# Decode attention with a gated feed-forward: K turned by VectorE in 32-bit blocks instead of by TensorE, one V slot, one set a loop turn

## The chip, the core and the metric

The kernel runs on one core of a Trainium2 chip. Engines: PE is TensorE (PEld its weight loads), DVE VectorE, ACT ScalarE, POOL GpSimd, SP the engine that issues most transfers. The metric is the device time of one execution in microseconds (us), as the median over runs.

## The reference

One new token for each of four batch rows goes through attention over the last 4096 positions of a cache, and beside it through a ReLU-gated feed-forward; a sigmoid gate of the token mixes the two. All tensors are bfloat16.

```python
g = sigmoid((A_x * gate_w).sum(-1, keepdims=True))      # A_x: 4 x 1 x 512
q = (A_x @ A_wq) as 32 heads of 128                      # A_wq: 512 x 4096
k, v = last 4096 positions of A_k_cache, A_v_cache       # 4 x 8 heads x 16384 x 128
p = softmax(q . k * 128 ** -0.5)                         # 4 query heads share one k/v head
a = (p . v) @ A_wo                                       # A_wo: 4096 x 512
h = relu(A_x @ W_gate) * (A_x @ W_up)                    # 512 x 1792 each (the token is A_x)
b = h @ W_down                                           # 1792 x 512
out = g * a + (1 - g) * b
```

## The kernel before, in words

The attention is cut into eight sets: batch row b = s // 2 and four of the eight k/v heads. A set's K is 4 MB and lies in SBUF as 128 partitions of 32 KB; so does its V. Both have two slots (`Ksb[:, s % 2]`, `Vsb[:, s % 2]`), which the weights reuse: W_q in the second V slot at the start, W_gate and W_up in the first K slot and W_down in the first V slot at the end. W_o has a place of its own (`Wbig`).

SP issues all large transfers in one fixed order: W_q, K0, K1, V0, K2, V1, ..., K7, V6, W_gate, W_up, V7, W_down, W_o in five pieces. They are served first in, first out. A K load waits until the scores of the set two back have read its slot, a V load until the value products two back have.

For each set, the positions must come onto the partitions' other side, since scores contract over the 128 elements of a head. Two bf16 elements are taken as one 32-bit word, and PE turns the K of a set in 64 fp32 transposes of 128x128 words (L352), eight to a fill of a PSUM buffer; two buffers alternate, and ACT and DVE copy the fills back over K in SBUF (L357, L359). Then:

- scores (L373): 32 products of 512 columns in two halves, four abreast in 32-column groups of PE; DVE adds a mask and takes the row maximum (L383);
- maximum (L390, L395): one product brings the maxima of all partitions into one row, DVE reduces it;
- exponent (L403) on ACT over 128x2048, turn (L413): DVE transposes the weights in 32x32 blocks;
- values (L421): 64 products of 256 columns, four abreast; ACT copies the sums out (L430).

The softmax and the value products of set s-1 are interleaved by hand with the transposes and scores of set s. PE's program is a loop of four turns of two sets each (the first set of a turn carries the end of the set before), the other engines' programs are straight lists. After the loop come the last set's rest, `combine` (L440 to L448: sums over partitions, normalising), `gateup` and the feed-forward's elementwise steps (L457 to L470), and the products with W_down and W_o (L503), 256 columns each and two abreast, into one PSUM bank; DVE and ACT copy the result (L517, L518) and SP writes it.

Before the loop: the gate's sigmoid, the projection of the queries (L310: 32 products of 512 columns, four abreast), and the queries' layout (L320 to L340; L340 is POOL's copy of one set's queries).

Of the kernel before, what the change touches and what calls it, by code (L numbers as in the profile page):

```python
# [11 lines left out]
B = 4  # L12
D = 512
HQ = 32
HKV = 8
SK = 16384
DH = 128
# [5 lines left out]
SCALE = DH ** -0.5  # L23
NEG = -1.0e9
LOWEST = -3.0e38

NTR = 2
NPAIR = 2
NFILL = 8
WO_CUTS = (0, 16, 26, 30)  # L30
ACT_TAKES = (1, 3, 4, 6, 7)


class Program:

# [8 lines left out]
    def __init__(self):  # L44
        self.ops = {e: [] for e in self.ENGINES}
        self.events = {}
        self.counts = {}
        self.history = {}
        self.dmas = []
        self.turns = []  # L50
        self.shared = {}
# [37 lines left out]
    def per_turn(self):  # L89

        return self.lowered

    def emit_list(self, eng, sems, engine, ops, shift, seen):
        for fn, name, waits, is_dma in ops:
            for s, n in self.need(engine, waits).items():
# [10 lines left out]
    def signature(self, ops, shift):  # L106
        seen = {}
        out = []
        for fn, name, waits, is_dma in ops:
# [9 lines left out]
    def emit(self, engine, eng, sems):  # L119
        ops = self.ops[engine]  # L120
        if engine != "pe":
            self.emit_list(eng, sems, engine, ops, {}, {})
            return
        t = self.turns
        self.emit_list(eng, sems, engine, ops[:t[0]], {}, {})
        first = self.signature(ops[t[0]:t[1]], {})
        for k in range(1, len(t) - 1):
            shift = {s: k * n for s, n in self.lowered.items() if s not in self.shared}
            assert self.signature(ops[t[k]:t[k + 1]], shift) == first, k
# [5 lines left out]
        shift = {s: (len(t) - 1) * n for s, n in self.lowered.items() if s not in self.shared}  # L135
        self.emit_list(eng, sems, engine, ops[t[-1]:], shift, {})


def bass_gated_mix__sliding_block_cached__glu_gated_reglu__decode_kernel(
# [13 lines left out]
    with ExitStack() as ctx:  # L153
        def sb(name, shape, dt):
            return ctx.enter_context(nc.sbuf_tensor(name, shape, dt))

        Ksb = sb("Ksb", [128, 2, 16384], BF16)
        Vsb = sb("Vsb", [128, 2, 16384], BF16)
        Wbig = sb("Wbig", [128, 16384], BF16)
        sc = sb("sc", [128, 2, 2048], BF16)  # L160
        pT = sb("pT", [128, 2, 2048], BF16)
        qrow = sb("qrow", [128, 2, 1024], BF16)
        mask = sb("mask", [128, 1024], BF16)
        ident = sb("ident", [128, 128], BF16)
        identw = sb("identw", [128, 128], FP32)
        ones = sb("ones", [128, 128], BF16)
        onesf = sb("onesf", [128, 132], FP32)
        Wsel = sb("Wsel", [128, 132], FP32)
        Wsum = sb("Wsum", [128, 64], FP32)
        m4 = sb("m4", [128, 20], FP32)  # L170
        S32 = sb("S32", [128, 32], FP32)
        xsb = sb("xsb", [5, 512], BF16)
        xT = sb("xT", [128, 4, 32], BF16)
        xw = sb("xw", [5, 512], FP32)
        gwB = sb("gwB", [128, 512], BF16)
        gsb = sb("gsb", [128, 8], FP32)
        qW = sb("qW", [128, NSET, 2, 32], BF16)
        qS = sb("qS", [128, 2, 2, 32], BF16)
        mx = sb("mx", [128, 2, NPAIR], FP32)
        mrow = sb("mrow", [128, 128], FP32)  # L180
        qmask = sb("qmask", [128, 128], FP32)
        negmax = sb("negmax", [128, 2], FP32)
        rowsum = sb("rowsum", [128, NSET], FP32)
        osb = sb("osb", [128, NSET, 256], FP32)
        recip = sb("recip", [128, 4], FP32)
        rgate = sb("rgate", [128, 4], FP32)
        idle = sb("idle", [128, 2], FP32)
        oq = sb("oq", [128, 128], BF16)
# [396 lines left out]
```

## Time and profile before

| | |
|---|---|
| median of 3 runs | 196.26 us (196.18 to 196.35) |
| profiled execution, its own time | 196.16 us |
| its span | 194.9 us |
| PE busy | 129.2 us (66%), 1578 products |
| DVE busy | 73.8 us (38%) |
| ACT busy | 66.5 us (34%) |
| POOL busy | 11.7 us (6%) |
| read from HBM | 81.01 MB, 416 GB/s over the span |

The time of an execution is that of the runs; every row of the profile comes from the one profiled execution, and its span runs from the first to the last record. In a row of a group: line, engine, operation, what is written and read, shape, count, then busy time in us and mean ns of one, then the idle time of the engine just before them and what ended it. In a row of the timeline: start, length (both us), engine, line, operation. PEclk is the clock granted to PE, 1.00 being full.

### The profile page before, as it was taken

Reading aid. Unit: us, or ns where it says so; the run is one execution under the profiler, and the core shown is the slowest. Engines: PE = TensorE matmul, PEld = TensorE weight load, DVE = VectorE, ACT = ScalarE, POOL = GpSimd, SP = SyncE. Lnnn points to the kernel's source line nnn. Section 1 sums busy time; section 2 is a strip of 40 time slices with the busy share of each in tenths; the row PEclk is TensorE's granted clock in tenths of the full one; section 3 lists DMA queues with packets and bytes.
Section 4 is the critical chain, followed back from the end, with each engine's and each line's share of the span. In section 5 each row is a group of like instructions: output and inputs, shape, how many; then the busy total and the mean of one; then the engine's idle time right before and its main releaser. Section 6 shows DMA issues by size and latency. Waiting matters only on the chain.

```text
span 194.9 us, 3496 instructions
## 1 busy us (share of the span) xinstructions
PE 129.2 (66%) x1578; PEld 101.0 (52%) x1578; DVE 73.8 (38%) x95; ACT 66.5 (34%) x77; POOL 11.7 (6%) x43
## 2 busy tenths in 40 slices
PE   0137398788769649872887099649972987713964
PEld 0113396576556439651765097439651865503742
DVE  0200045259239323930682029324920492180000
ACT  2005025565255452435342424433435252510000
POOL 8820000000000000000000000000000000000000
PEclk9999999999999996999999859996999699995799
DMA  6999999999999999999999999999999999998992
GB/s 216 431 430 437 430 430 427 437 440 430 437 440 430 437 430 437 430 430 437 432 437 425 430 437 430 430 437 430 430 430 430 430 390 427 475 430 382 424 403 82
DMA packets 3881, 81.11 MB, mean 416 GB/s; under 512 B 409, under 2 KB 930, under 8 KB 1058
## 3 DMA queue, kind: packets, MB, share of 16 engines
q1 hardware_dynamic: 3864, 81.01, 97.3%
q8 instruction: 5, 0.08, 0.2%
q14 instruction: 2, 0.02, 0.0%
q10 hardware_dynamic: 10, 0.01, 0.0%
HBM read 81.01 MB, written 0.00 MB: 416 GB/s over the span
## 4 chain that ended last, share of the span: by engine, by line
DMA 59%; PE 21%; DVE 14%; ACT 3%; issue 1%; SPq 1%
DMA Ksb<-in_A_k_cache_dram 47%; PE TRT L352 15%; DMA Wbig<-in_A_wo_dram 12%; DVE Ksb L359 6%; DVE pT L413 5%; PE SCT L373 3%; DVE sc L383 3%; ACT Ksb L357 3%; PE OB L421 2%; PE SCT L503 1%; SPq L240 0%; PE FB L390 0%; SPq L533 0%; ACT outr L518 0%; SPq L235 0%
## 5 line engine op out<-in xcount | busy, mean ns | idle before, releaser
L352 PE MATMUL TRT<-identw,Ksb 128*128 128x128 f32 x512 | 75.1, 306 | 25.4 <-DMA Ksb<-in_A_k_cache_dram 17.5
L352 PEld LDWEIGHTS TRT<-identw,Ksb 128*128 128x128 f32 x512 | 65.9, 158 | 35.8 <-DMA Ksb<-in_A_k_cache_dram 18.8
L357 ACT COPY Ksb<-TRT 128x1024 f32<-128x1024 f32 x40 | 40.5, 1012 | 58.4 <-PE TRT L352 58.2
L359 DVE COPY Ksb<-TRT 128x1024 f32<-128x1024 f32 x24 | 29.4, 1223 | 40.1 <-PE TRT L352 40.1
L421 PE MATMUL OB<-Vsb,pT 128*32 128x256 bf16 x576 | 19.0, 288 | 7.5 <-DMA Vsb<-in_A_v_cache_dram 7.5
L373 PE MATMUL SCT<-Ksb,qS 128*32 128x512 bf16 x256 | 16.9, 381 | 8.8 <-ACT Ksb L357 8.8
L421 PEld LDWEIGHTS OB<-Vsb,pT 128*32 128x32 bf16 x576 | 16.4, 101 | 10.4 <-issue 7.9
L383 DVE CUSTOM_DVE_ANT_0 sc<-SCT,mask,mx 128x1024 bf16<-128x1024 f32 x8 | 10.3, 1284 | 26.9 <-PE SCT L373 26.9
L403 ACT ACTIVATE sc<-sc,negmax 128x2048 bf16<-128x2048 bf16 x8 | 16.0, 2002 | 10.7 <-DVE negmax L395 10.7
L413 DVE STREAM_TRANSPOSE pT<-sc 128x2048 bf16<-128x2048 bf16 x8 | 18.4, 2302 | 2.2 <-ACT sc L403 2.2
L430 ACT COPY osb<-OB 128x256 f32<-128x256 f32 x8 | 3.0, 372 | 31.1 <-PE OB L421 31.1
L373 PEld LDWEIGHTS SCT<-Ksb,qS 128*32 128x32 bf16 x256 | 5.2, 94 | 15.7 <-ACT Ksb L357 11.6
L383 DVE CUSTOM_DVE_ANT_0 sc<-SCT,mask 128x1024 bf16<-128x1024 f32 x8 | 9.8, 1225 | 2.2 <-PE SCT L373 2.2
L340 POOL COPY qS<-qW 128x64 bf16<-128x64 bf16 x8 | 1.8, 238 | 113.3 <-PE SCT L373 105.2
L390 PE MATMUL FB<-identw,mx 128*128 128x128 f32 x18 | 4.7, 343 | 5.7 <-issue 5.7
L395 DVE CUSTOM_DVE_ANT_0 mrow<-FB,qmask 128x128 f32<-128x128 f32 x8 | 2.3, 292 | 12.8 <-PE FB L390 12.8
L390 PEld LDWEIGHTS FB<-identw,mx 128*128 128x128 f32 x18 | 2.9, 200 | 7.6 <-issue 7.6
L292 PE MATMUL FB<-identw,xw 5*128 5x5 f32 x4 | 0.6, 262 | 8.5 <-POOL m L267 8.5
L503 PE MATMUL SCT<-Wbig,oq 128*4 128x256 bf16 x64 | 4.3, 273 | 2.6 <-DMA Wbig<-in_A_wo_dram 2.6
L310 PE MATMUL SCT<-Vsb,xT 128*32 128x512 bf16 x32 | 3.6, 631 | 2.8 <-DMA Vsb<-in_A_wq_dram 2.8
L292 PEld LDWEIGHTS FB<-identw,xw 5*128 5x128 f32 x4 | 0.6, 207 | 8.5 <-DVE xw L286 8.5
L503 PEld LDWEIGHTS SCT<-Wbig,oq 128*4 128x4 bf16 x64 | 2.7, 87 | 4.2 <-DMA Wbig<-in_A_wo_dram 3.6
(61 smaller groups left out, 42.7 us busy)
## 6 DMA issues: line engine op xcount, KB each, us to landing
Ksb<-in_A_k_cache_dram SPq DMA_DIRECT2D x8, 4096.0 KB, 24.2
Vsb<-in_A_v_cache_dram SPq DMA_DIRECT2D x8, 4096.0 KB, 32.2
Vsb<-in_A_wq_dram SPq DMA_DIRECT2D x1, 4096.0 KB, 12.3
Wbig<-in_A_wo_dram SPq DMA_DIRECT2D x1, 2048.0 KB, 21.5
Ksb<-in_B_W_gate_dram SPq DMA_DIRECT2D x1, 1792.0 KB, 19.7
Ksb<-in_B_W_up_dram SPq DMA_DIRECT2D x1, 1792.0 KB, 23.6
Vsb<-in_B_W_down_dram SPq DMA_DIRECT2D x1, 1792.0 KB, 17.0
Wbig<-in_A_wo_dram SPq DMA_DIRECT2D x1, 1280.0 KB, 24.1
```

The source lines that it names most:

```text
L310: P.op("pe", lambda e, half=half, t=t, g=g, col=col: e.matmul(SCT[32 * g:32 * g + 32, 512 * half:512 * half + 512], xT[:, t, :], Wq3[:, t, ...
L352: P.op("pe", lambda e, bk=bk, cc=cc, c=c: e.transpose(bk[:, cc * 128:(cc + 1) * 128], Kw[:, s % 2, c * 128:(c + 1) * 128], identw[:, :]), ...
L357: P.op("act", lambda e: e.copy(dst, bk), ("KTC", s, i), [("KT", s, i)], sem="va")
L359: P.op("dve", lambda e: e.tensor_copy(dst, bk), ("KTC", s, i), [("KT", s, i)], sem="vd")
L373: P.op("pe", lambda e, a=a, o=o, hb=hb, bank=bank: e.matmul(SCT[32 * a:32 * a + 32, 512 * hb:512 * hb + 512], qS[:, s % 2, o, :], k4[:, 16 ...
L383: P.op("dve", lambda e: e.tensor_tensor_reduce(sc[:, s % 2, pair * 1024:(pair + 1) * 1024], SCT[:, :], mask[:, :], 1.0, mx[:, s % 2, 0:1] ...
L390: P.op("pe", lambda e: e.matmul(FB[:, 384:512], mx[:, par, 1:2].to_broadcast([128, 128]), identw[:, :], start=True, stop=True), ("MT", s), ...
L403: P.op("act", lambda e: e.activation(sc[:, par, :], sc[:, par, :], ACTF.Exp, bias=negmax[:, par:par + 1], scale=SCALE, accum_out=rowsum[:, ...
L413: P.op("dve", lambda e: e.transpose(pT[:, par, :], sc[:, par, :]), ("PTT", s), [("EXP", s), ("PV", s - 2) if s >= 1 else None], sem="vd")
L421: P.op("pe", lambda e, g=g, blk=blk: e.matmul(OB[32 * g:32 * g + 32, 0:256], pT[:, par, 32 * blk:32 * blk + 32], Vsb[:, par, 256 * blk:256 ...
L430: P.op("act", lambda e: e.copy(osb[:, s, :], OB[:, 0:256]), ("OSB", s), [("PV", s)], sem="va")
L503: P.op("pe", lambda e: e.matmul(AB[32 * u:32 * u + 4, 0:256], stat, mov[:, 256 * u:256 * u + 256], start=start, stop=stop, tile_position=( ...
```

## The change

K is no longer turned by PE. DVE turns it with two transposes a set, each of 128x4096 32-bit words in blocks of 32x32, into a buffer `KT` of its own; the scores then read `KT`. Because only 32x32 blocks are turned, the 128 elements of a head are spread differently, and the queries, the softmax weights and the value products are laid out for that: the queries are kept in zero-padded strips (`qz`, `qS`), the scores of a set fit one PSUM bank of 128x512 (`SB`) and need no mask, the weights are permuted by one product with a permutation matrix (`perm`, L369), copied out by ACT, transposed by DVE (L375) and spread into a zero-padded buffer `pm` by two copies on DVE and two on ACT (L379). The value products are 32 of 512 columns, two abreast in 64-column groups (L387). DVE masks and sums what belongs together (L391, L394), one product adds over partitions (L396), and the set is normalised at once (L400 to L403) instead of in `combine`.

V has one slot: the load of V(s) waits for the value products of set s-1. W_gate, W_up and W_down have places of their own and wait for nothing; W_o is loaded into `KT` after the last scores. The loads take K and V with partition = (head, block of positions) instead of (block, head).

PE's loop has one set a turn, eight turns; a branch inside it runs `gateup` in the last turn alone, between the permutation and the value products. The programs of PE, DVE, ACT and POOL are each wrapped in a body that runs once, with a branch hint, and each program fits into two blocks of instructions. At the end, W_down and the first 20 blocks of W_o are taken by products of 512 columns with a stationary operand 36 columns wide, the rest as before.

The diff, cut to its core (nearly all lines of the kernel function differ; left out are the constants, the queries' layout and the feed-forward's elementwise steps, which compute what they did):

```diff
@@ Program.emit: PE's loop, and the body that runs once
-        with eng.Fori(0, len(t) - 1):
-            self.emit_list(eng, sems, engine, ops[t[0]:t[1]], {}, {})
-            eng.drain()
-            for s, n in self.lowered.items():
-                eng.sem_inc(sems[s], -n)
+        with self.once(nc, engine, eng):
...
+            with nc.body("pe_loop", valid_engines=bass.OrderedEngineSet([eng.engine])):
+                self.emit_list(eng, sems, engine, ops[t[0]:t[1]], {}, {}, turn)
+                eng.drain()
+                for s, n in self.lowered.items():
+                    eng.sem_inc(sems[s], -n)
+                eng.reg_add(turn, turn, 1)
+                eng.br_lt(turn, len(t) - 1, on_true="pe_loop", on_false="pe_loop_end")
@@ loads
         def load_k(s):
             P.dma("sp", lambda e: e.dma_start(Ksb[:, s % 2, :], heads(A_k_cache, s)), ("K", s),
-                  [("SC", s - 2, NPAIR - 1)] if s >= 2 else [], sem=loop_sem("K", s))
+                  [("KTC", s - 2, 1)] if s >= 2 else [])
 
         def load_v(s):
-            P.dma("sp", lambda e: e.dma_start(Vsb[:, s % 2, :], heads(A_v_cache, s)), ("V", s),
-                  [("PV", s - 2)] if s >= 1 else [], sem=loop_sem("V", s))
+            P.dma("sp", lambda e: e.dma_start(Vsb[:, :], heads(A_v_cache, s)), ("V", s),
+                  [("PV", s - 1) if s else ("Q",)], sem="V")
@@ K's transposes, scores, softmax, values
-        def kt(s, i):
-            ...
-                P.op("pe", lambda e, bk=bk, cc=cc, c=c: e.transpose(
-                    bk[:, cc * 128:(cc + 1) * 128], Kw[:, s % 2, c * 128:(c + 1) * 128], identw[:, :]),
-                    ("KT", s, i) if cc == 7 else None, w)
+        def turned(s, u):
+            lo = 4096 * u
+            P.op("dve", lambda e: e.transpose(KT[:, lo:lo + 4096], Kw[:, s % 2, lo:lo + 4096]), ("KTC", s, u),
+                 [("K", s), ("SC", s - 1, u) if s else None], sem="vd")
...
+        def scores(s):
+            for u in range(2):
+                for v in range(2):
+                    for o in range(2):
+                        for g in range(4):
+                            m = g + 4 * u
+                            last = v == 1 and o == 1
+                            P.op("pe", lambda e, u=u, v=v, o=o, g=g, m=m, last=last: e.matmul(
+                                SB[32 * g:32 * g + 32, :], qS[:, 2 * v + o, 16 - 16 * u:48 - 16 * u],
+                                Kt[:, 16 * m:16 * m + 16, v, :, o], start=(u == 0 and v == 0 and o == 0),
+                                stop=(u == 1 and last), tile_position=(0, 32 * g)),
+                                ("SC", s, u) if (last and g == 3) else None, [("KTC", s, u), ("QS", s)])
+
+        def softmax(s):
+            par = s % 2
+            P.op("dve", lambda e: e.tensor_reduce(mx[:, :], SB[:, :], AXIS.X, ALU.max), ("MX", s),
+                 [("SC", s, 1)], sem="vd")
+            P.op("pe", lambda e: e.matmul(FB[:, 128:256], mx[:, 0:1].to_broadcast([128, 128]), identw[:, :],
+                                          start=True, stop=True), ("MT", s), [("MX", s)])
             P.op("dve", lambda e: e.tensor_tensor_reduce(
...
+                ("NEGMAX", s), [("MT", s), ("QMASK",), ("EXP", s - 2) if s >= 2 else None])
             P.op("act", lambda e: e.activation(
+                p[:, :], SB[:, :], ACTF.Exp, bias=negmax[:, par:par + 1], scale=SCALE,
+                accum_out=rowsum[:, par:par + 1]), ("EXP", s), [("NEGMAX", s)], sem="va")
+            P.op("pe", lambda e: e.matmul(PB[:, :], perm[:, :], p[:, :], start=True, stop=True), ("PERM", s),
+                 [("EXP", s)])
+            P.op("act", lambda e: e.copy(pP[:, :], PB[:, :]), ("PTE", s), [("PERM", s)])
+            P.op("dve", lambda e: e.tensor_copy(
+                osum[:, 128:129], rowsum[:, par:par + 1]),
+                ("RS", s), [("EXP", s), ("SEL", s - 1) if s else None])
+            P.op("dve", lambda e: e.transpose(pT[:, :], pP[:, :]), ("PTT", s), [("PTE", s)])
+            for h in range(4):
+                r = slice(32 * h, 32 * h + 32)
+                eng = ("dve", "act")[h % 2]
+                P.op(eng, lambda e, h=h, r=r: (e.copy if h % 2 else e.tensor_copy)(
+                    pm[r, :].rearrange("p (m c q) -> p m c q", m=8, q=16)[:, :, :, 4 * h:4 * h + 4],
+                    pT[r, :].rearrange("p (c m j) -> p m c j", m=8, j=4)),
+                    ("PM", s, h), [("PTT", s), ("PM0",), ("PV", s - 1) if s else None], ...)
 
         def values(s):
+            for blk in range(32):
+                g = blk % 2
                 P.op("pe", lambda e, g=g, blk=blk: e.matmul(
+                    OB[64 * g:64 * g + 64, :], pm[:, 64 * blk:64 * blk + 64], Vsb[:, 512 * blk:512 * blk + 512],
+                    start=(blk < 2), stop=(blk >= 30), tile_position=(0, 64 * g)),
+                    ("PV", s) if blk == 31 else None, [("PM", s, 2), ("PM", s, 3), ("V", s)])
             P.op("dve", lambda e: e.tensor_tensor(
+                osb[:, :, :], OB[:, :].rearrange("p (e d) -> p e d", e=4),
+                emask[...].to_broadcast([128, 4, 128]), ALU.mult), ("OM", s), [("PV", s), ("EMASK",)])
+            P.op("dve", lambda e: e.tensor_reduce(osum[:, 0:128], osb[:, :, :].rearrange("p e d -> p d e"), AXIS.X, ALU.add),
+                 ("OSB", s), [("OM", s), ("SEL", s - 1) if s else None], sem="vd")
+            P.op("pe", lambda e: e.matmul(OS[0:16, 0:129], S16[:, :], osum[:, :], start=True, stop=True), ("SEL", s), [("OSB", s), ("S16",)])
@@ the order of the work
         for s in range(NSET):
+            load_q(s)
+            turned(s, 0)
+            turned(s, 1)
...
+            if s:
+                normal(s - 1)
+            P.turn_edge()
+            scores(s)
+            softmax(s)
+            P.op("pe", "aside")
+            if s == NSET - 1:
+                at = len(P.ops["pe"])
+                gateup()
+                P.aside = (at, len(P.ops["pe"]))
+                units()
+            values(s)
         P.turn_edge()
+        normal(NSET - 1)
...
+        down(0, WD_FIRST)
```

`normal(s)` is three DVE steps on the set's sums: a reciprocal (RC), a scaling of 16x128 (ON) and a transpose of 32x128 (OT).

More of the change, by code (lines that the diff above doesn't have):

```diff
@@ L1 @@
[L1 removed]
+from contextlib import ExitStack, contextmanager
 import concourse.bass as bass
@@ L120, in emit @@
+    def emit(self, nc, engine, eng, sems):
         ops = self.ops[engine]
-        if engine != "pe":
+        if engine == "sp":
             self.emit_list(eng, sems, engine, ops, {}, {})
             return
[L124 to L129, printed above, removed]
@@ L155, in sb, with ps @@
             return ctx.enter_context(nc.sbuf_tensor(name, shape, dt))
+        def ps(name, width):
+            return ctx.enter_context(nc.psum_tensor(name, [128, width], FP32))
         Ksb = sb("Ksb", [128, 2, 16384], BF16)
[L158 to L163, printed above, removed]
@@ new lines, in down @@
+        def down(lo, hi):
+            for i in range(lo, hi):
+                wide(hT[:, i:i + 35 * NFT + 1:NFT], Wd[:, i, :], i == 0, [("WD",), ("H",)])
+        down(0, WD_FIRST)
+        for b in range(4):
+            P.op("pe", lambda e, b=b: e.transpose(OS[:, 256 + 32 * b:288 + 32 * b], oT[:, b, 0:128], identw[0:32, 0:32]),
+                 ("CB",) if b == 3 else None, [("OT", NSET - 1), ("IDENTW",)])
+        P.op("dve", lambda e: e.tensor_copy(
+            oq[:, :].rearrange("p (k w) -> p k w", k=9)[:, 0:9:8],
+            OS[:, 256:384].rearrange("p (k w) -> p k w", k=1).to_broadcast([128, 2, 128])),
+            ("OQ",), [("CB",), ("OQ0",)], sem="vd")
```

505 lines of the change are left out of this document (201 added, 304 removed).

## Prediction

> **What bounds the kernel now.** I read the page's head, its DMA slices and the chain first.
>
> ```profile
> span 194.9 us, 3496 instructions
> DMA  6999999999999999999999999999999999998992
> DMA 59%; PE 21%; DVE 14%; ACT 3%; issue 1%; SPq 1%
> ```
>
> The transfers run at 90% or more in all slices but the first and the last few, and DMA holds 59% of the chain. The PE, DVE and ACT pieces of that chain lie in turns whose results freed a slot for a transfer already queued behind others. So the stream of bytes is the bound. Its pace comes from the timeline and the DMA issues:
>
> ```profile
> Vsb<-in_A_wq_dram SPq DMA_DIRECT2D x1, 4096.0 KB, 12.3
> 13.12 3.60 PE L310 MATMUL SCT<-Vsb,xT 128*32 128x512 bf16 x32 [2.84 <-DMA Vsb<-in_A_wq_dram]
> 22.82 7.79 PE L352 MATMUL TRT<-identw,Ksb 128*128 128x128 f32 x40 [3.35 <-DMA Ksb<-in_A_k_cache_dram]
> ```
>
> Two 4 MB blocks land at 13.12 and 22.82: 9.70 us a block, so one set (K and V) needs 19.40 us of stream. A block issued into an idle stream lands 12.3 after its issue. Compute needs at most 19.40 us a set to stay hidden; today it does, since PE transposes set s while DVE and ACT drain it.
>
> **The new loop.** The bytes are the same, so the question is the length of one turn of compute. The compiled order of the changed kernel puts on DVE, in this order, for each set: two transposes KTC of 128x4096 words, three small steps of the set before, MX, NEGMAX, RS, PTT, two PM copies, OM, OSB, and then the next set's KTC. DVE takes them in order. OM waits for PV, the value products of the same set; PV waits for PM; PM hangs on the scores of the same set's KTC. So nothing of set s+1 starts on DVE before PV of set s has ended: the turn is a closed ring, and its length is the sum of its links. Queued behind OM's wait are OSB and the next KTC, and PE's scores and the next K load wait for those.
>
> *KTC.* Before there is no 4096-word transpose. Nearest rows:
>
> ```profile
> L413 DVE STREAM_TRANSPOSE pT<-sc 128x2048 bf16<-128x2048 bf16 x8 | 18.4, 2302 | 2.2 <-ACT sc L403 2.2
> L469 DVE STREAM_TRANSPOSE hcol<-hrow 128x448 f32<-128x448 f32 x1 | 0.6, 646 | 0.0
> ```
>
> One line through both gives 1.035 ns an element and 0.18 fixed, whatever the width of the element. 4096 words are then 4.42 and the pair 8.84. Upper bound, the 448-word row scaled without a fixed part (1.44 ns a word): 11.8. I take 8.84, since both rows lie on it.
>
> *PE's clock.* The ring leaves PE idle most of a turn, and idle time has a price here:
>
> ```profile
> 163.81 1.92 PE L421 MATMUL OB<-Vsb,pT 128*32 128x256 bf16 x64
> 178.59 3.60 PE L421 MATMUL OB<-Vsb,pT 128*32 128x256 bf16 x64 [7.50 <-DMA Vsb<-in_A_v_cache_dram]
> core 0: us, PE busy (x) PEld busy (x) DVE busy (x) ACT busy (x) POOL busy (x), PEclk, DMA share, GB/s
> 107.30:110.70 3.40, 0.00 (x0) 0.00 (x0) 0.05 (x2) 2.10 (x2) 0.00 (x0) 1.00 0.94 405
> 110.70:114.10 3.40, 2.48 (x12) 2.48 (x13) 0.47 (x1) 0.00 (x0) 0.00 (x0) 0.50 0.96 414
> 114.10:117.50 3.40, 3.40 (x18) 3.39 (x17) 1.21 (x2) 1.01 (x1) 0.00 (x0) 0.50 1.01 434
> 148.25:151.67 3.42, 1.19 (x11) 1.19 (x12) 0.06 (x1) 1.13 (x2) 0.00 (x0) 1.00 1.00 431
> 151.67:155.08 3.41, 3.41 (x18) 3.19 (x16) 1.35 (x2) 1.01 (x1) 0.00 (x0) 0.50 1.03 442
> 178.96:182.37 3.41, 3.23 (x63) 2.33 (x52) 0.00 (x0) 0.13 (x1) 0.00 (x0) 0.50 1.02 434
> 182.50:183.00 0.50, 0.34 (x3) 0.34 (x4) 0.00 (x0) 0.11 (x1) 0.00 (x0) 1.00 0.98 393
> 185.78:189.20 3.42, 2.03 (x38) 1.45 (x36) 0.00 (x0) 0.00 (x0) 0.00 (x0) 1.00 1.00 420
> ```
>
> The same 64 products take 1.92 after work and 3.60 after 7.5 us of idling. The granted clock (sixth figure) changes on a grid of 3.41 us. A window with 35% PE work (148.25) is followed by half clock, one with 59% (185.78) is kept at full. At half clock, 73% (110.70) is not enough to get full clock back, 95% (178.96) is. In the ring PE rests through OM, OSB and the first KTC, 5.8 us, whose windows cannot hold 35% work. So every turn's scores start at half clock, and so does PV, with PTE, PTT and PM (2.6 us without PE work) just ahead of it.
>
> [...]
>
> *The PE links.*
>
> ```profile
> L310 PE MATMUL SCT<-Vsb,xT x32: 607/634/634, 13.1 to 16.1; 128*32 128x512 bf16 x32
> L373 PE MATMUL SCT<-Ksb,qS x256: 376/378/400, 30.5 to 163.6; 128*32 128x512 bf16 x128
> 162.93 1.05 PE L373 MATMUL SCT<-Ksb,qS 128*32 128x512 bf16 x16 [1.10 <-ACT Ksb L357]
> 18.69 0.77 PE L390 MATMUL FB<-identw,mx 128*128 128x128 f32 x2
> 167.02 0.48 PE L390 MATMUL FB<-identw,mx 128*128 128x128 f32 x2 [1.30 <-issue]
> ```
>
> A 512-column product takes 0.634 at half and 0.378 at full clock. The 32 of L310 run four abreast: eight rounds, (3.60-0.634)/7 = 0.424 a round; at full clock (1.05-0.378)/3 = 0.22. The second half of the scores (four rounds; the first half hides under the second KTC): 3x0.424+0.634 = 1.91, at full 1.05. MT, the same transposing product: 0.77, full 0.48. PERM, one product of 512 columns: 0.63, full 0.38. PV is 32 products of 512 columns, two abreast, 16 rounds: all at half clock 15x0.424+0.634 = 7.0, all at full 15x0.22+0.38 = 3.7. The clock returns at the end of the first well-filled window, 2.9 to 6.3 us after PV starts (needing about 85%), 4.6 in the middle: 3.7+4.6/2 = 6.0.
>
> *The DVE and ACT links.*
>
> ```profile
> L359 DVE COPY Ksb<-TRT 128x1024 f32<-128x1024 f32 x24 | 29.4, 1223 | 40.1 <-PE TRT L352 40.1
> L517 DVE CAST outr<-SCT 4x256 bf16<-4x256 f32 x1 | 0.4, 411 | 7.5 <-PE SCT L503 7.5
> L357 ACT COPY Ksb<-TRT 128x1024 f32<-128x1024 f32 x40 | 40.5, 1012 | 58.4 <-PE TRT L352 58.2
> L320 ACT CAST qrow<-SCT 128x512 bf16<-128x512 f32 x4 | 2.1, 600 | 5.8 <-PE SCT L310 5.8
> 167.54 0.29 DVE L395 CUSTOM_DVE_ANT_0 mrow<-FB,qmask 128x128 f32<-128x128 f32 x1 [2.21 <-PE FB L390]
> 167.88 2.00 ACT L403 ACTIVATE sc<-sc,negmax 128x2048 bf16<-128x2048 bf16 x1 [1.73 <-DVE negmax L395]
> 170.00 2.31 DVE L413 STREAM_TRANSPOSE pT<-sc 128x2048 bf16<-128x2048 bf16 x1 [2.16 <-ACT sc L403]
> 72.72 0.04 issue
> ```
>
> MX, OM and OSB pass 512 elements each: between 0.411 (256) and 1.223 (1024), 0.68 apiece. NEGMAX to the start of EXP: 0.34. EXP on 512: 2.00 less 1536 times 0.80 ns (1.012-0.600 over 512) = 0.77, and 0.12 until the next starts = 0.89. PTE 0.60. PTT: 0.18+0.53 = 0.71. PM: ACT's two copies of 512, 0.52+0.60 = 1.12, beside DVE's. Nine hand-overs of 0.04: 0.4. RS hides under PERM and PTE, the three small steps under the scores; uncovered they cost under 1.0.
>
> Sum of the ring: 8.84+1.91+0.68+0.77+0.34+0.89+0.63+0.60+0.71+1.12+6.0+0.68+0.68+0.4 = **24.25 us** against 19.40 of stream. The other moves cost nothing while the ring is that long. V's single slot: V(s) is issued when PV(s-1) ends, lands 12.3 later, and is wanted 1.4+8.84+8.0 = 18.3 later. K(s+2) is issued at KTC(s)'s end, more than a turn ahead. One set a turn of PE's loop: the drain and the branch lie under the first KTC.
>
> ```profile
> L340 POOL COPY qS<-qW 128x64 bf16<-128x64 bf16 x8 | 1.8, 238 | 113.3 <-PE SCT L373 105.2 <-DVE qW L334 8.1
> q8 instruction: 5, 0.08, 0.2%
> q14 instruction: 2, 0.02, 0.0%
> ```
>
> The new way of the queries (two copies of 0.7, a transpose of 1.2, nine POOL copies near 0.24) ends about 21 after the projection's 16.7, and the scores want it at 27.2. Keeping each program within two instruction blocks can save what fetches take from the stream, 0.2% of it: 0.4 us, and nothing while the ring is the bound. If the fetches at the loop's branch were late, the 5.8 us of rest would cover them.
>
> **The whole time.** K(0) lands at 22.82 and V(0) by 22.82+19.40 = 42.22; set 0's PM is ready at 22.82+8.84+8.0 = 39.7, so PV(0) starts at 42.2 and OSB(0) ends at 42.2+6.0+1.4 = 49.6. Seven turns more: 49.6+7x24.25 = 219.4. In the last turn gate-up runs between PERM and PV: eight rounds of 448 columns at half clock, 8x0.37 = 3.0, against 2.6 that PE would idle. PV(7) starts 0.4 late, with 1.6 of the 4.6 cold instead of all, which saves 1.5: 218.3. The tail:
>
> ```profile
> 184.62 1.69 PE L503 MATMUL SCT<-Vsb,hT 128*4 128x256 bf16 x28
> 184.73 0.19 DVE L445 RECIPROCAL recip<-TRT 64x4 f32<-64x4 f32 x1 [10.10 <-PE TRT L443]
> 185.14 0.29 DVE L448 TENSOR_TENSOR oq<-TRT,rgate 64x128 bf16<-64x128 f32 x1
> 190.81 2.37 PE L503 MATMUL SCT<-Wbig,oq 128*4 128x256 bf16 x32 [1.19 <-DMA Wbig<-in_A_wo_dram]
> 193.22 0.36 ACT L518 CAST outr<-SCT 4x256 bf16<-4x256 f32 x1 [10.60 <-PE SCT L503]
> ```
>
> SEL about 0.5, the three normalising steps about 0.8 (0.70 for the like three at 184.73 to 185.43), four small transposes 0.5: 1.8. Thirty wide products behind them, 30x0.22 = 6.6. Twenty-four narrow ones, two abreast, by L503's 0.11 a round: 1.5. From PE's last product to the end 194.9-193.2 = 1.7. Sum 11.6. W_o, issued when KT is free (195.1+8.84+1.91 = 205.9), lands behind V(7) and W_down at about 220, hidden by 2 us. Span 218.3+11.6 = 229.9. The profiled execution took 196.16 for a span of 194.9, so 231.2; the median shown is 0.10 above it: **231 us**.
>
> **Rivals.**
> *PE stays at full clock* (its work counts for more than the busy rows say). The ring is 24.25-0.86-0.29-0.25-2.3 = 20.5, still over 19.40: 42.2+3.7+1.4+7x20.5+11.6+1.3 = 204. Against it: the 3.60 at 178.59.
> [...]
> *Words turn slower than halfwords*, up to 11.8 a pair: seven turns 3.0 longer and PV(0) 0.4 later, up to 253. Against it: the one line through two rows.
> *The ring fits under the stream, and the kernel is faster.* One place decides: the KTC pair at full clock must take under 8.84-(20.5-19.4) = 7.7 us, as if DVE moved about two words a cycle. Then the stream is the bound, ends as now near 190.8, and only the shorter finish (1.5 for 2.37) shows: about 195.3. Against it: the 0.646 for 448 words, and the half clock, which alone pushes the point down to 4.0.
>
> **How the numbers follow.** Measurement tells about 0.2% apart here. Forecast 0.75; full clock 0.06; the idle-window rule 0.07; slower words 0.08; faster 0.04, of which a quarter too little to tell. The forecast's own range, with PV's warming between 2.9 and 6.3 (0.85 a turn either way) and half a microsecond a turn unknown in OSB's strided read, is 222 to 241. The range given adds the idle-window rule, part of the slower words and of the warmer clock: 212 to 246. Chances: faster 0.03, same 0.01, slower 0.96.
>
> **What would show it.** Right: KTC rows near 4.4 us with the next KTC starting right after OSB; turns of 24 us; DMA slices falling to about 8 tenths with gaps; PE's clock at half in most of a turn; PV near 6 us; OM's wait on PV among the longest. Wrong: KTC off 4.4; PV at 3.7 with clock 1.00; the DMA line still all nines with turns of 19.4.

## The result, and the profile after

The changed kernel takes 805.3 us (799.96 to 814.23, four runs) against 196.22 us (196.05 to 196.35) for the kernel before: a ratio of 4.095, interval 4.075 to 4.116. The forecast was 231 us in 212 to 246. The side was right, the size was not nearly. A ratio can leave out a single run that is off the others (here 814.23 us), so it isn't always the quotient of the times beside it.

The page of the changed kernel, the lines that answer to those shown of before (DMA is the busy share of 16 engines in tenths, GB/s what they moved, in 40 slices of 20 us):

```profile
span 803.1 us, 1738 instructions
PEclk9999999999955555556555655555555555555557
DMA  6222222222222222222222222222227422584220
GB/s 235 52 59 59 60 67 65 72 73 82 86 96 104 108 109 108 108 108 108 109 108 109 108 108 108 108 109 108 109 108 176 129 109 107 134 170 87 60 81 30
q1 hardware_dynamic: 3816, 81.01, 29.9%
another core or an unknown queue 72%; DVE 11%; PE 10%; issue 2%; DMA 2%; ACT 1%; PEld 1%; ACTq 0%; PEldq 0%; DVEq 0%
L387 PE MATMUL OB<-Vsb,pm 128*64 128x512 bf16 x256 | 47.8, 555 | 521.9 <-DMA Vsb<-in_A_v_cache_dram 521.9
L341 DVE STREAM_TRANSPOSE KT<-Ksb 128x4096 f32<-128x4096 f32 x16 | 70.1, 4419 | 60.3 <-DMA Ksb<-in_A_k_cache_dram 60.3
```

The first slice holds W_q at 6 tenths; from the second, where K starts, the DMA line stands at 2 tenths and the rate at 52 GB/s. It creeps to 108 in 250 us and stays there. The bytes are those of before (81.01 MB). PE waits 521.9 us for V in eight waits, and the engines' own work is small: the two groups of PE and DVE here are 47.8 and 70.1 us of 803. The 72% of the chain that has no name are such waits for transfers. The windows say it exactly; the last two columns are the DMA share and GB/s:

```profile
40.00:60.00 20.00, 0.00 (x0) 0.00 (x0) 0.00 (x0) 0.00 (x0) 0.00 (x0) 1.00 0.25 57
320.00:340.00 20.00, 0.00 (x0) 0.00 (x0) 0.00 (x0) 0.00 (x0) 0.00 (x0) 0.50 0.25 108
```

A share of 0.25 is four engines of sixteen, all the time busy. The trace's single packets (it keeps each one's start, length and size, but not its engine) bear that out: from 20 to 600 us four rows of 32 KB are in flight at nearly any time, where the kernel before has sixteen. So the transfers of K and V, not the loop, set the time. Two questions follow: why four engines, and why four engines at first give half of what they give later.

The suspect for the first is one word order in `heads()`, which names the axes of the load. Before it reads `"r h (c d)"`, with 32 blocks of positions outermost; after, `"h r (c d)"`, with 4 heads outermost. An estimate from the two traces: the outermost axis of a load sets how many engines share it, up to all sixteen. With 32 outermost sixteen rows are in flight; with 4 outermost it is four, at a share of 0.25.

### The profile page after: what moved, and what is told of

Its sections match the earlier page's. It is cut to its first block, busy times and chain, and to the rows that moved or that the text cites. A ratio compares the mean times of both kernels' runs of the same rounds, so it can differ in the third digit from the quotient of the medians.

```text
span 803.1 us, 1738 instructions
## 1 busy us (share of the span) xinstructions
PE 112.2 (14%) x680; PEld 44.9 (6%) x680; DVE 114.5 (14%) x125; ACT 25.1 (3%) x47; POOL 14.4 (2%) x34
## 2 busy tenths in 40 slices
DMA packets 3856, 81.01 MB, mean 101 GB/s; under 512 B 268, under 2 KB 784, under 8 KB 1040
## 3 DMA queue, kind: packets, MB, share of 16 engines
q1 hardware_dynamic: 3816, 81.01, 29.9%
HBM read 81.01 MB, written 0.00 MB: 101 GB/s over the span
## 4 chain that ended last, share of the span: by engine, by line
another core or an unknown queue 72%; DVE 11%; PE 10%; issue 2%; DMA 2%; ACT 1%; PEld 1%; ACTq 0%; PEldq 0%; DVEq 0%
DVE KT L341 8%; PE OB L387 5%; DMA xs<-in_gate_w_dram 2%; PE SB L351 2%; PE AB L452 1%; DVE osum L394 1%; PE FB L361 1%; DVE mx L359 1%; ACT p L366 1%; DVE osb L391 1%; PE PB L369 1%; PE QG L317 0%; PEld OB L387 0%; ACTq L255 0%
## 5 line engine op out<-in xcount | busy, mean ns | idle before, releaser
L387 PE MATMUL OB<-Vsb,pm 128*64 128x512 bf16 x256 | 47.8, 555 | 521.9 <-DMA Vsb<-in_A_v_cache_dram 521.9
L391 DVE TENSOR_TENSOR osb<-OB,emask 128x512 f32<-128x512 f32 x8 | 5.5, 692 | 553.1 <-PE OB L387 553.1
L341 DVE STREAM_TRANSPOSE KT<-Ksb 128x4096 f32<-128x4096 f32 x16 | 70.1, 4419 | 60.3 <-DMA Ksb<-in_A_k_cache_dram 60.3
L387 PEld LDWEIGHTS OB<-Vsb,pm 128*64 128x64 bf16 x256 | 23.0, 157 | 547.3 <-issue 545.2
L351 PE MATMUL SB<-KT,qS 128*32 128x512 bf16 x256 | 30.4, 623 | 114.0 <-DVE KT L341 114.0
L351 PEld LDWEIGHTS SB<-KT,qS 128*32 128x32 bf16 x256 | 7.2, 126 | 132.9 <-DVE KT L341 124.2
L379 ACT COPY pm<-pT 32x512 bf16<-32x512 bf16 x16 | 9.8, 615 | 6.9 <-DVE pT L375 6.7
L394 DVE TENSOR_REDUCE osum<-osb 128x128 f32<-128x512 f32 x8 | 8.2, 1019 | 0.3
L452 PE MATMUL AB<-Wd,hT 128*36 128x512 bf16 x14 | 6.2, 616 | 0.9 <-PEq L151 0.9
L369 PE MATMUL PB<-p,perm 128*128 128x512 bf16 x8 | 4.9, 608 | 9.6 <-ACT p L366 9.6
L375 DVE STREAM_TRANSPOSE pT<-pP 128x512 bf16<-128x512 bf16 x8 | 5.6, 702 | 0.0
L396 PE MATMUL OS<-osum,S 128*16 128x129 f32 x16 | 3.1, 278 | 14.7 <-DVE osum L394 14.7
L379 DVE COPY pm<-pT 32x512 bf16<-32x512 bf16 x16 | 4.5, 284 | 0.5
```

The source lines that it names most:

```text
L341: P.op("dve", lambda e: e.transpose(KT[:, lo:lo + 4096], Kw[:, s % 2, lo:lo + 4096]), ("KTC", s, u), [("K", s), ("SC", s - 1, u) if s else ...
L351: P.op("pe", lambda e, u=u, v=v, o=o, g=g, m=m, last=last: e.matmul(SB[32 * g:32 * g + 32, :], qS[:, 2 * v + o, 16 - 16 * u:48 - 16 * u], ...
L369: P.op("pe", lambda e: e.matmul(PB[:, :], perm[:, :], p[:, :], start=True, stop=True), ("PERM", s), [("EXP", s)])
L375: P.op("dve", lambda e: e.transpose(pT[:, :], pP[:, :]), ("PTT", s), [("PTE", s)])
L379: P.op(eng, lambda e, h=h, r=r: (e.copy if h % 2 else e.tensor_copy)(pm[r, :].rearrange("p (m c q) -> p m c q", m=8, q=16)[:, :, :, 4 * h: ...
L387: P.op("pe", lambda e, g=g, blk=blk: e.matmul(OB[64 * g:64 * g + 64, :], pm[:, 64 * blk:64 * blk + 64], Vsb[:, 512 * blk:512 * blk + 512], ...
```

## Experiments: the load order, and what else it could be

The theory (A) is that the head-outermost order alone makes the 805. The rivals: (B) the single V slot leaves the stream without work; (C) the heads lie 4 MiB apart in memory, and loads at that distance are slow.

**The kernel before with that one edit.** It keeps its PE transposes and its two V slots; K and V lie otherwise than its masks and copies read them.

```diff
-            return ... .rearrange("h (r c) d -> r h (c d)", r=32)
+            return ... .rearrange("h (r c) d -> h r (c d)", r=32)
```

> The kernel before with one edit: K and V are loaded with the head outermost, as in the change (the positions then lie on other partitions than the scores take them for, so its output means nothing; its work is the same). Theory A: 16 blocks of 4.19 MB at 4 engines, 108 GB/s at best (39 us a block): 700 to 800 us, DMA share 0.25 for most of the span. Rival B (the single V slot): stays at 196.

Measured: 765.5 us, ratio 3.904 (3.896 to 3.911). Its page:

```profile
span 763.7 us, 3496 instructions
DMA  6222222222222222222222222222225252228721
GB/s 242 57 57 64 63 66 70 67 76 77 85 94 103 106 108 110 106 110 106 109 108 110 105 108 108 110 108 106 110 108 156 108 156 110 106 107 206 170 108 64
```

The same twos, the same creeping from 57 to 108. One word order turns 196 into 766; all the rest of the change adds 40 us to that, by what is not shown. This kernel has two V slots, so (B) does not make the 805; (A) stands.

**The heads 4 KB closer in memory.** The sources in the changed kernel's loads start 4 MiB less 4 KiB apart instead of 4 MiB, so that it reads other positions.

```diff
-            return cache[b, 4 * half:4 * half + 4, SK - WIN:SK, :].rearrange("h (r c) d -> h r (c d)", r=32)
+            flat = cache[b, 4 * half:4 * half + 4, :, :].rearrange("h s d -> (h s d)")
+            far = SK * 128 - 2048
+            return flat[0:4 * far].rearrange("(h x) -> h x", h=4)[:, 0:WIN * 128].rearrange("h (r c) -> h r c", r=32)
```

> The changed kernel, but the four heads of a load are read at a pitch of 4 MiB less 4 KiB, from the start of the cache (other positions and mixed heads, so its output means nothing; the transfers keep their shape, 4 heads outermost). Theory A alone: the DMA share stays 0.25 and the rate still creeps from 52 to 108 GB/s: 800 us. A with collision of the four equal-phase streams (C as a second cause): 108 GB/s from the start, 67 MB in 621 us, all in 660 to 700. C alone as the cause: far faster than that, above 108 GB/s.

Measured: 795.46 us (one run; 805.3 unedited, whose own runs spread over 14 us). The rate again begins at 53 and ends at 106 to 112. At this distance too, then, the rate is what it was: (C) is out as far as 4 KB can tell.

**The changed kernel with the old order.** Only the word order goes back; K and V then lie as the old kernel had them, not as the scores read them, but every instruction and byte is the changed kernel's. It is the kernel that the prediction had in mind.

```diff
-            return ... .rearrange("h (r c) d -> h r (c d)", r=32)
+            return ... .rearrange("h (r c) d -> r h (c d)", r=32)
```

> The changed kernel with one edit: K and V are loaded in one transfer with the 32 row blocks outermost and the 4 heads inside, as the kernel before loads them (rows then lie on other partitions than the scores take them for, so its output means nothing; its work is the same). It spreads a transfer over all engines and all partitions at once. Theory: the per-head loads lost half the rate because all engines wrote into the same 32 partitions (DMA share 1.00 at 210 GB/s); here the stream is back at 430, and the ring of the prediction, with the links as the changed kernel's trace has them (24.6 us a turn), sets the time: 50+7x24.6-1+14 and 1.4 outside the span: 237 us (233 to 240). Rival, transfers issued one at a time from one V slot cost rate whatever their shape: 300 or more. Rival, the ring overlaps more than the compiled order shows: 200 to 215.

Measured: 233.51 us (232.57 to 234.39), ratio 1.1905 (1.1863 to 1.1947). Its page and, below, one turn from DVE's timeline and the value products from PE's:

```profile
span 231.3 us, 1738 instructions
DMA  7999999999995989499959994999598946989600
```

```profile
71.91 0.69 DVE L391 TENSOR_TENSOR osb<-OB,emask 128x512 f32<-128x512 f32 x1 [6.13 <-PE OB L387]
72.64 1.02 DVE L394 TENSOR_REDUCE osum<-osb 128x128 f32<-128x512 f32 x1
73.57 8.76 DVE L341 STREAM_TRANSPOSE KT<-Ksb 128x4096 f32<-128x4096 f32 x2
84.34 0.69 DVE L359 TENSOR_REDUCE mx<-SB 128x1 f32<-128x512 f32 x1 [1.10 <-PE SB L351]
88.42 0.70 DVE L375 STREAM_TRANSPOSE pT<-pP 128x512 bf16<-128x512 bf16 x1
```

```profile
66.54 5.34 PE L387 MATMUL OB<-Vsb,pm 128*64 128x512 bf16 x32 [2.81 <-ACT pm L379]
82.39 1.90 PE L351 MATMUL SB<-KT,qS 128*32 128x512 bf16 x16 [2.43 <-DVE KT L341]
85.09 0.80 PE L361 MATMUL FB<-identw,mx 128*128 128x128 f32 x2 [0.80 <-DVE mx L359]
90.51 5.30 PE L387 MATMUL OB<-Vsb,pm 128*64 128x512 bf16 x32 [2.81 <-ACT pm L379]
```

The next KTC starts right behind the second sum (the records overlap by 0.1), and from one PV to the next are 23.97 us. The ring of the prediction exists as described; in the changed kernel it lies hidden under transfers that take 38.8 us a block at 108 GB/s. PE's clock in this kernel falls to half in every turn:

```profile
PEclk9999755595559655875587557855695569558769
```

## Experiments: four engines, and half of their rate

**Four transfers a set instead of one.** Each head goes alone, so that its 32 rows are outermost and by that estimate 16 engines take part.

```diff
+            for h in range(4):
+                P.dma("sp", lambda e, h=h: e.dma_start(Ksb[32 * h:32 * h + 32, s % 2, :], heads(A_k_cache, s)[h]), ...
```

(and so for V)

> The changed kernel, but each K and V load is issued as four transfers, one for each head, of 32 rows of 32 KB (the changed kernel issues one transfer whose outermost dimension is the 4 heads). Theory A, few engines: an outermost dimension of 4 puts a transfer on 4 of the 16 DMA engines (the DMA share was 0.25 wherever only K and V moved); with 32 rows outermost the stream is back at about 430 GB/s, and the turn of compute is what is left: 24.6 us a turn by the links of the changed kernel's own trace, 50+7x24.6 and a tail of 12 to 15: 232 to 238 us. Rival B, one V slot: the loads are slow because one at a time is issued with nothing queued behind it; then this stays near 800. Rival C, the heads' addresses lie 4 MiB apart and the four streams collide in HBM: this reads one head at a time and gains too, so it doesn't tell A from C.

Measured: 367.53 us (363.38 to 369.54), ratio 1.878 (1.868 to 1.887): far from 232. The page:

```profile
span 361.5 us, 1778 instructions
DMA  8999999999999999999999999999999999998992
GB/s 334 305 203 203 228 196 214 218 192 228 214 192 232 207 199 228 196 214 218 192 228 214 192 232 207 199 228 196 214 218 196 225 214 192 315 323 174 268 415 100
q1 hardware_dynamic: 4776, 81.01, 98.0%
```

All sixteen engines are busy and move half of what they could: a row of 32 KB takes 2.49 us on average, where it takes 1.21 at full rate. That makes 190 to 230 GB/s, where the row-first kernel reaches over 400. A busy DMA line is no full rate. A new rival pair: the 32 neighbouring partitions into which all engines write (D), or transfers of 1 MB as such (E). The same kernel with 50 idle products of PE a turn, to keep the clock up, was to show the ring at full clock, but the transfers cover it:

```diff
+        def warm(n, s):
+            for k in range(n):
+                P.op("pe", lambda e: e.matmul(AB[:, :], perm[:, :], qrow[:, 0:512], start=True, stop=True), None, [("QS", s)])
```

(called six times a turn, 16 + 13 + 2 + 4 + 9 + 6)

> The per-head loads, with 50 idle products of 512 columns a turn on PE (into the bank that only the end uses) in the gaps before and between the scores, around the two small products and ahead of the value products. If PE's half clock is the price that the prediction put on the ring (3.8 us a turn): the value products take 3.7 instead of 6.0, the turn 20.8, in all about 206 us. If the turn is held by something else, 230 or more; if the extra products themselves come in the way, slower than the per-head kernel.

Measured: 365.94 us, at a granted clock of 0.794 (0.608 without); no change, as the transfers set the time.

**The same transfers, other partitions.** Against the kernel of four transfers a set, only the destination rows differ:

```diff
-   ... Ksb[32 * h:32 * h + 32, s % 2, :], heads(A_k_cache, s)[h] ...
+   ... Ksb[h:128:4, s % 2, :], heads(A_k_cache, s)[h] ...
```

> The per-head kernel (four 1 MB transfers a set, 32 rows each, the same count and the same bytes, 367.5 us) with one thing changed: the 32 rows of a head are written to every fourth partition (h, h+4, h+8, ...) instead of 32 neighbouring ones. The output is then meaningless, the work is not. If the half rate (210 GB/s at a DMA share of 1.00) comes from 16 engines writing into one run of 32 partitions, the rate returns to about 430 GB/s, the turn to the 23.9 us of the ring, and the time to that of the row-first kernel, 234 us (232 to 238). If it comes from the size or the number of the transfers, it stays at 362 to 370 us.

Measured: 232.79 us (232.24 to 233.33), ratio 1.187 (1.183 to 1.190).

```profile
span 231.6 us, 1786 instructions
GB/s 272 453 436 402 430 453 447 419 407 441 362 396 260 436 362 453 181 407 390 379 226 407 362 441 192 385 390 402 272 362 370 428 198 272 453 372 410 259 0 1
```

Full rate, with the same number and size of transfers, and again 32 partitions each: (D) is shown, (E) is out. What slows a transfer is not how many partitions it writes but which ones: some 210 GB/s into 32 neighbouring ones, over 400 into every fourth. Why is not shown.

**Engines out of step.** The changed kernel, with 20 loads of 14 KB a row ahead of K0 into the place of W_down, ten of one row and ten of three. By the estimate above they go to one engine and to three, and of the four engines the first and second then run some 140 KB apart, and so do the third and fourth.

```diff
+        for k in range(20):
+            n, lo = (1, k) if k < 10 else (3, 3 * k - 20)
+            P.dma("sp", lambda e, n=n, lo=lo: e.dma_start(
+                Wd[lo:lo + n, :, :].rearrange("p i w -> p (i w)"),
+                A_k_cache[0, 0:n, 0:56, :].rearrange("h a d -> h (a d)")), ("SCR", k))
```

(and W_down's own load waits for them)

> The changed kernel with 20 small extra loads of 14 KB a row ahead of K0 (10 on one engine, 10 on three), so that the four engines that carry K and V start about 140 KB apart in pairs. It computes the same. The four engines began at 52 GB/s and needed some 250 us to reach 108 GB/s, which is 27 GB/s an engine, what each of sixteen gives at 430. If that is two engines writing rows r of two heads 32 partitions apart at the same moment, the offset gives 108 GB/s from the first block on: 64 MB of K and V and 4 MB of W_q at 108 to 112 GB/s and the rest as before, 660 to 710 us. If the creeping has another cause (a warming of the memory or of the engines), 795 to 815 us.

Measured: 732.74 us (one run).

```profile
span 731.5 us, 1768 instructions
DMA  6222222222222222222222222222283221972210
GB/s 265 107 108 108 109 108 108 108 108 108 111 109 108 108 108 109 108 108 108 108 109 109 109 108 108 109 108 108 108 194 125 109 107 81 180 160 61 70 63 22
```

108 GB/s from the second slice on, where the changed kernel had 52. So four engines that start row r of four heads together hold one another up, give half of 4 x 27 GB/s, and drift apart over 250 us.

The packets show how. In the changed kernel most rows take 2.4 to 2.57 us from 40 to 60 us, in two pairs of nearly equal lengths (2.56 and 2.57 beside 2.48 and 2.49). From 260 us on a row takes 1.21. The packets that close a block on its four engines then come at 285.3, 286.0, 290.0 and 290.8 us: two and two lie 4.7 us apart, about four rows, and so they do in the blocks that follow. With the offset the four engines begin K0 at 12.76, 18.19, 18.60 and 23.30 us, steps near the 5.3 that ten rows of 14 KB take at 27 GB/s, and from 25 us on a row takes 1.21. The two in the middle, by the extra loads those of heads 1 and 2, begin 0.41 us apart and don't slow each other, so being in step is not enough.

So the loss arises between certain heads, and 1 and 2 are no such pair. Which heads pair is not shown, as the trace doesn't say which engine a packet used; nor is what the two of a pair share, or why about four rows between them are enough.

The expected time, 660 to 710, was missed by over 20 us: that estimate took the end at an even pace, and the line shows 60 to 80 GB/s in several of the last slices.

**Two tries at a fast load in the new layout.** First, heads 0 and 1 on SP's queue and 2 and 3 on ACT's, with DVE's order opened (below):

```diff
+        def load_k(s, q=0):
+            for h in (0, 1) if not q else (2, 3):
+                P.dma(("sp", "act")[q], lambda e, h=h: e.dma_start(Ksb[32 * h:32 * h + 32, s % 2, :], ...
```

> A version that computes the reference with this layout: the opened order, and each K and V load as four transfers of one head, heads 0 and 1 (partitions 0 to 63) from SP's queue and heads 2 and 3 (partitions 64 to 127) from ACT's. If the per-head loads were held by the partitions that they all wrote at one time, the two queues reach twice as many and the rate is back near 430: 197 to 205 us. If they were held by their size or their number (1 MB each, twice the issues), it stays at 210 GB/s and 360 us.

Measured: 352.92 us (350.56 to 356.84), ratio 1.795 (1.788 to 1.803). The rate stays at 190 to 240 GB/s with the DMA line at nines. A second queue feeds the same sixteen engines: at nearly all times 16 packets are in flight in all, never 32, and mostly nearly all of them belong to one of the two queues, which take turns. So the engines mostly still write into one head's 32 partitions together.

Second, one queue, heads in the order 0, 2, 1, 3 in two column halves each, and the first two heads of K0 cut into pieces of 15 rows down to 1, meant to give each second engine 32 KB more than the next (the trace doesn't say which engine carries which row):

```diff
+        HALVES = [(h, 0, 32, 8192 * c, 8192 * c + 8192) for c in range(2) for h in (0, 2, 1, 3)]
+        SKEW = [(0, 0, 15, 0, 16384), (0, 15, 28, 0, 16384), (0, 28, 31, 0, 16384), (0, 31, 32, 0, 16384),
+                (1, 0, 11, 0, 16384), (1, 11, 20, 0, 16384), (1, 20, 27, 0, 16384), (1, 27, 32, 0, 16384)]
...
```

> Computes the reference in the layout of the change, with the opened DVE order. K and V go as eight 512 KB transfers a set on SP's queue (two halves of the columns, heads in the order 0, 2, 1, 3), and the first two heads of K0 are cut into pieces of 15, 13, 11, 9, 7, 5, 3 and 1 rows, which give each second engine 32 KB more than the next. [...] If the half rate is two engines writing the same few partitions of one half at once, this brings the rate back to 400 GB/s and more, and the time to that of the row-first kernel with the opened order, 205.3 us, and up to 5 us a few times over for the engine that carries the most: 206 to 225 us. If pieces of 32 partitions are slow however the engines stand, or if the queues run dry and the engines fall into step again, it stays at 330 to 370 us.

Measured: 346.76 us (343.8 to 350.96), ratio 1.774 (1.763 to 1.786): no remedy. The windows show how it went:

```profile
30.00:40.00 10.00, 0.00 (x0) 0.00 (x0) 0.00 (x0) 0.00 (x0) 3.57 (x8) 0.53 0.98 180
60.00:70.00 10.00, 1.92 (x12) 0.89 (x5) 6.13 (x8) 2.59 (x5) 0.34 (x1) 0.50 1.01 362
70.00:80.00 10.00, 5.98 (x32) 2.84 (x32) 5.28 (x3) 0.00 (x0) 0.00 (x0) 0.58 0.73 282
80.00:90.00 10.00, 2.69 (x36) 1.45 (x37) 5.79 (x13) 2.59 (x5) 0.35 (x1) 0.76 0.99 228
```

Once the cut K0 is through (at 180 GB/s), the rate climbs to 362. At 70 to 80 the queue runs dry while V(1) waits for PV(0) (share 0.73), and from then on it is about 220 to 230 through the loop. The packets fit engines that fall into step when they start again together: a 16 KB piece takes some 0.72 us from 56 to 74 us, fewer and fewer are in flight up to 80, nine pieces of V(1) start between 80.64 and 80.82, and from 82 on a piece takes 1.15 to 1.2. The gain lasted until the queue ran dry.

## Experiments: the loop itself

With the row-first loads the forecast's clock and order can be tried.

**PE kept warm.** The 50 idle products of `warm` above, at the same six places of the turn.

> The row-first loads of the kernel beside it (output means nothing for the same reason), with 50 idle products of 512 columns a turn on PE in the gaps of the ring, which keep its clock up. If half the clock costs the 3.8 us a turn that the prediction put on it: a turn of 20.8, 47.7+7x20.8+13+1.4: 207 us (203 to 214). If the ring doesn't set the time, no change from the row-first kernel.

Measured: 212.79 us (212.62 to 212.86), ratio 1.0848 (1.0833 to 1.0863), clock 0.984 for 0.690. PE's timeline, with PV at 3.64 for 5.3:

```profile
107.91 3.64 PE L397 MATMUL OB<-Vsb,pm 128*64 128x512 bf16 x32 [0.82 <-DVE pm L388]
129.06 3.64 PE L397 MATMUL OB<-Vsb,pm 128*64 128x512 bf16 x32 [0.82 <-DVE pm L388]
```

The turn is 21.15 us: 2.8 less than at the low clock, 20.7 us over the whole.

**The ring opened.** KTC of the next set goes ahead of OM and OSB (`sums`) on DVE. The selecting product and the normalising steps of a set move behind the next set's scores, and those of the last set behind W_down's products. In short:

```diff
+            else:
+                sums(s - 1)
...
+            select(s - 1)
```

> The row-first loads (output means nothing for the same reason) with DVE's order changed: both transposes of set s+1 are issued ahead of the two steps that wait for the value products of set s, and the selecting product and the normalising steps move behind the next scores; at the end all W_down products go ahead of the selecting product. The ring is opened: transposes 8.7, scores 1.9 and the softmax links 6.2 make 17 us a turn, under the stream's 19.4. If the closed ring is what holds the row-first kernel, the stream sets the time again: 196 to 202 us, with a longer finish than the kernel before. If it is the single V slot, V(s) waits for value products that end 6 to 7 us after V(s-1) landed, against 9.7 of K's transfer less 2.6 of issue: no room for error, 202 to 215.

Measured: 205.32 us (205.07 to 208.85), ratio 1.0464 (1.0448 to 1.0481). PE's and SP's timelines:

```profile
101.78 5.65 PE L387 MATMUL OB<-Vsb,pm 128*64 128x512 bf16 x32 [8.90 <-DMA Vsb<-in_A_v_cache_dram]
122.12 5.72 PE L387 MATMUL OB<-Vsb,pm 128*64 128x512 bf16 x32 [8.68 <-DMA Vsb<-in_A_v_cache_dram]
```

```profile
107.46 0.53 SPq L249 DMA_DIRECT2D Vsb<-in_A_v_cache_dram  x1
108.19 0.54 SPq L245 DMA_DIRECT2D Ksb<-in_A_k_cache_dram  x1
```

And its page:

```profile
span 203.6 us, 1742 instructions
DMA  6999999999999999999999999999998998999930
```

The turn is 20.34. PV ends at 107.43, V is issued at 107.46 and lands at 122.12: the chain now runs through the single V slot, PV plus a landing of 14.7. That is 0.9 a turn over the stream's 19.40. But the engines hardly rest: their share over this turn and the next is 1.01 and 0.99, at 427 and 417 GB/s. So whether the slot or the pace of the transfers makes the 0.9 is not shown. Of the 9 us over the kernel before, some 4.3 lie in the finish: 17.0 us follow the last PV (186.6 to 203.6), for 12.7 there (182.2 to 194.9).

**Both.** The opened order with 28 idle products a turn ahead of PV:

```diff
+            warm(28, s)
```

> The row-first loads with the opened DVE order (205.3 us) and 28 idle products of PE in each turn ahead of PV, to keep the granted clock up. Only the compute side is read, its output is meaningless like that of the row-first kernel. The single V slot's turn there was 20.4 us: 12 us of landing behind the last PV product, then the transposes, the exchange and PV. If the clock rises to 0.95 and over, a PV of 5 us takes about 2.6 and V is asked for 2 us earlier, so that the turn falls to the stream's 19.4 us: 205.3 - 8 turns x 1.0 - 3 to 4 us of a faster tail = 193 to 199 us. If the idle products only push PV later, the turn grows by their time: 205 to 212 us.

Measured: a ratio of 1.0256 (1.0207 to 1.0304); four of five runs at 200.02 to 202.01 us, clock 0.91 to 0.96. Between what the two cases expected; the 2 us over the first stay open. No kernel here beats the one before, even with the loads at full rate.

## Why the prediction was wrong

The step that failed is the first sentence of the loop's part: "The bytes are the same, so the question is the length of one turn of compute." The bytes are the same, their pace is not. The 9.70 us a block and the 12.3 from issue to landing were carried over from before, although the loads' order had changed; the forecast costed that edit at nothing, gave no reason, and had no rival for it. In their place stand 52 to 108 GB/s, 38.8 us a block at best. The edit is worth some 570 us by itself (196.1 to 765.5 in the kernel before). Everything that hung on this pace fell with it: V's single slot (landing 12.3 after its issue, wanted 18.3 after it), K "more than a turn ahead", W_o "hidden by 2 us", and the sign by which it was to be known, a DMA line of 8 tenths (it stands at 2).

Right, and covered by the slow stream: with the old order the kernel takes 233.5 us for a forecast of 231, with turns of 23.97 for 24.25, and a DMA share of 0.84 over the span (the line at 8 tenths that was to be the sign). That the two times lie so close is in part luck: from the end of the first OSB to that of the last it takes 2.8 us less than forecast (165.9 for 168.7), and the finish takes 15.7 us (215.6 to 231.3) for 11.6. The finish was mis-sized mostly because the fourteen W_down products run at half clock, 6.3 us in all or 0.45 each, where the forecast gave a wide product 0.22.

- KTC: 8.76 a pair for 8.84. The line through a 2048- and a 448-element row held up to 4096 words, and the rival of slower words is out.
- PV: 5.3 for 6.0, inside the given 3.7 to 7.0.
- OSB: 1.02 for 0.68. It reads in strides and writes 128 sums; MX passes as many elements in order into one and takes 0.69. Which of the two costs the half again is not shown.
- Scores 1.90 for 1.91, MX and OM 0.69 for 0.68, MT 0.80 for 0.77, PTT 0.70 for 0.71.
- The low clock: right, in every turn. No run shows the idle-window rule that the chances and the range count: from 73.42 to 76.83 PE does 0.39 us of work (SEL), 11% of the window, and the clock falls all the same (the scores at 78.06 take 1.90, their length at half clock). Holding it up saves 20.7 us of the 27 that the full-clock rival gave (204 for 231). For its 20.5 us a turn, 21.15 were seen, with idle products on PE.
- The rival of a faster kernel asked for less than its words say: 7.7 us a pair is 0.90 ns a word beside the fixed 0.18, an eighth under the line's 1.035, and no run gives DVE's cycle, by which it counts "two words". At 8.76 a pair it is out all the same.

## What to carry to other kernels

Read a reordered load as a changed load: look at which dimension is outermost and how many partitions, how far apart, are written at one moment, before carrying a landing time over. The new layout gained nothing here, as no load tried filled it at full rate. And look at the rate beside the busy share: here 0.25 was twelve engines missing, and 1.00 at half the rate was sixteen engines writing into 32 neighbouring partitions.

## What the runs showed of the hardware that was not expected

- One engine gives about 27 GB/s (32 KB in 1.21 us): four give 108, sixteen over 400. Four engines that start the same row of four heads hold one another up in two pairs (52 to 57 GB/s for the four), and drift apart by themselves only in some 250 us, until about four rows lie between the two of a pair.
- Sixteen engines writing into 32 neighbouring partitions move 210 GB/s at a share of 1.00; the same transfers over every fourth partition reach 453 in the best slice.
- The granted clock that the profile gives for the start of a run can be wrong. In the changed kernel its first record lies at 211.6 us, and all windows before read 1.00, those with work too (PEclk is the third figure from the end). Yet the scores at 92.52 take 1.90, the length of half clock, where sixteen of them took 1.05 at full clock in the kernel before:

```profile
85.00:95.00 10.00, 1.90 (x16) 0.45 (x16) 6.98 (x2) 0.00 (x0) 0.00 (x0) 1.00 0.26 66
92.52 1.90 PE L351 MATMUL SB<-KT,qS 128*32 128x512 bf16 x16 [66.91 <-DVE KT L341]
```
